# Where the tail of a rounded weight lies: two halves in PSUM, or one buffer in SBUF

## The chip, the core and the metric

The kernel runs on one core of a Trainium2 chip. The metric is the device time of one execution in microseconds (us): the lower the better. A core has TensorE (PE: matmuls and, beside them, PEld: the loads of their stationary operand), VectorE (DVE), ScalarE (ACT), GpSimd (POOL) and SyncE (SP), which here only issues DMAs. Each engine works through its own instructions in program order; semaphores hold an instruction until what it needs is done. SBUF is the working memory, PSUM the memory into which TensorE writes.

## What is computed

A linear attention with a decaying state (RWKV-6), for 4 batches, 8 heads, 768 tokens and a head size of 48, and then a two-layer network with SiLU on its output:

```python
for t in range(S):
    kt, vt, rt, wt = (k[:, :, t], v[:, :, t], r[:, :, t], w[:, :, t])
    cur = np.einsum('bhd,bhe->bhde', u[None] * kt, vt)
    y[:, :, t] = np.einsum('bhd,bhde->bhe', rt, state + cur)
    state = wt[:, :, :, None] * state + np.einsum('bhd,bhe->bhde', kt, vt)
x = y.transpose(0, 2, 1, 3).reshape(3072, 384)
h = x @ w_in                                   # 384 x 2048
g = h * (1.0 / (1.0 + np.exp(-h)))
out = g @ w_out                                # 2048 x 384
```

w_in and w_out come in as float64, everything else as float32. The kernel rounds the two weight matrices to float32 itself, from the two 32-bit words of each number. That rounding is what the change touches.

## The kernel before

The 768 tokens are cut into 6 blocks of 128; with 2 batches at a time this makes 12 **units**, `units[i]`. The attention of a unit (`mix(i)`) turns w, r and k so that channels lie on the partitions, and then goes through 7 **levels** (`level(i, l)`), in which the blocks of tokens that interact double in length. A level has 16 matmuls on TensorE (L377) that make scores; VectorE copies the masked scores out (L386, two of them), and multiplies r by the decay (L395, two inputs in SBUF); ScalarE copies half of the keys on (L365), and GpSimd multiplies the other half by the decay (L414, two of them). The next level's matmuls need L395, L365 and L414. In unit 1 GpSimd also has L333 and L334 (`bonus`), in unit 2 and later L322 (`products`).

The network of a unit has 8 steps `up(i, m)` (12 matmuls L549 each, SiLU on ScalarE at L552) and steps `down` (L559 for unit 0; for later units `quarter`, L604). `up(0, m)` is the first to use the m-th part of w_in, `down(0, ...)` the first to use w_out.

`merge` sets one program order for everything: each list of steps gets a stretch of a common time line, with unit i's attention at about i to i+1. The roundings of the 16 pieces of weight (0 to 7 of w_in, 8 to 15 of w_out) are put in at 0.6, from 1.0 to 1.83 and from 1.85 to 2.4, that is beside the levels of units 1 and 2; so are the steps `up(0, m)`, and `down(0, ...)` from 2.4 on.

One piece is 128 x 768 numbers of 64 bits. `round_weight(i)` issues, in this order: the add of any piece that is joined (`add_weight`), the join of piece i-1, the split of piece i, and the loads of later pieces into a place that is free by then.

- `split_weight(i)`: VectorE masks the high words into `head` (L169); ScalarE converts 16 bits of every number to `tail` (L173) and then works `head` over in place (L175). `head` lies in `temps[:, 0, i % 2]` in SBUF; `tail` in two PSUM tiles `p_o` of 384 columns, of which there are two in all.
- `join_weight(i)`: for each half, VectorE adds the low words to the tail in place (L189) and puts the sign bit on (L191), into `low`, `temps[:, 2, i % 2]` in SBUF.
- `add_weight()`: GpSimd adds `head` and `low`, both in SBUF, into the weight's place in `w_in_sb` or `w_out_sb` (L201). It is called ahead of each join and at the end of each level.

`temps` has room for three kinds of buffer, twice each; the kind with index 1 is not used by the rounding before. `p_o` is also the tile in which `down` and `quarter` gather their results, from `down(0, ...)` on. The later sums of Strassen's form (L578, L586) begin after the roundings.

Of the kernel before, what the change touches and what calls it, by code (L numbers as in the profile page):

```python
# [8 lines left out]
F32 = mybir.dt.float32  # L9
I8 = mybir.dt.int8  # L10
U16 = mybir.dt.uint16
U32 = mybir.dt.uint32
AF = mybir.ActivationFunctionType
ALU = mybir.AluOpType
# [19 lines left out]
def kernel(  # L34
# [11 lines left out]
    nc = tc.nc  # L46

    B, H, S, D = r.shape
    DM, DF = moe_w_in.shape
# [21 lines left out]
    ps = ctx.enter_context(tc.tile_pool(name="ps", bufs=1, space=bass.MemoryType.PSUM))  # L71
# [50 lines left out]
    PW = 2 * DM  # L122
# [17 lines left out]
    def staged(i):  # L140
        place = PLACES[i] - NOWN
        if place < 0:
            return own[:, PLACES[i]]
        return w_out_sb[:, 4 * place:4 * place + 4, :].rearrange("p a d -> p (a d)").bitcast(U32)
# [18 lines left out]
    half = {}  # L163
    temps = const.tile([128, 3, 2, PW], U32, name="temps")

    def split_weight(i):
        hi = staged(i)[:, 1::2]
        head = temps[:, 0, i % 2]
        nc.vector.tensor_scalar(out=head, in0=hi, scalar1=0x7FFF0000, scalar2=None, op0=ALU.bitwise_and)  # L169

        tails = [ps.tile([128, DM], F32, name="p_o", bufs=2) for x in range(PW // DM)]
        for x, tail in enumerate(tails):
            nc.scalar.activation(out=tail, in_=staged(i).bitcast(U16)[:, 2::4][:, x * DM:(x + 1) * DM],  # L173
                                 func=AF.Copy, scale=8.0)
        nc.scalar.activation(out=head, in_=head, func=AF.Relu, scale=8.0, bias=shift)  # L175
        half[i] = head, tails

    def join_weight(i):
        head, tails = half.pop(i)
        lo, hi = staged(i)[:, 0::2], staged(i)[:, 1::2]  # L180
        dst = w_ends[i][0].bitcast(U32)
        low = temps[:, 2, i % 2]

        def like(t):
            return t.rearrange("p (c f) -> p c f", c=dst.shape[1])

        for x, tail in enumerate(tails):
            part = slice(x * DM, (x + 1) * DM)
            nc.vector.scalar_tensor_tensor(out=tail.bitcast(U32), in0=lo[:, part], scalar=2.0 ** -29, in1=tail,  # L189
                                           op0=ALU.mult, op1=ALU.add)  # L190
            nc.vector.scalar_tensor_tensor(out=low[:, part], in0=hi[:, part], scalar=0x80000000, in1=tail.bitcast(U32),  # L191
                                           op0=ALU.bitwise_and, op1=ALU.bitwise_or)
        joined.append((dst, like(head), like(low)))

    joined = []
# [7 lines left out]
    def round_weight(i):  # L203

        add_weight()
        if rounded and 0 < i <= 2 * NW:
            join_weight(i - 1)
        if rounded and i < 2 * NW:
            split_weight(i)
        for j in due.get(i, ()):  # L210
            load_weight(j)
# [32 lines left out]
    for x, (c, p) in enumerate(parts):  # L244
        for e in range(2):
            first, rows = (2 * p + e) * D, slice(PD * e, PD * e + D)
            d0, d1 = max(0, c * 128 - first), min(D, (c + 1) * 128 - first)
            if d0 < d1:
                nc.scalar.copy(out=dense[rows, x, first + d0 - c * 128:first + d1 - c * 128],
                               in_=ident[rows, PD * e + d0:PD * e + d1])  # L250
# [4 lines left out]
    for l in range(NL):  # L255
# [3 lines left out]
        for b, sign in ((0, 1), (1, -1)):  # L259

            base, part = b * (L - 1), m[:, b]
# [428 lines left out]
```

## Time and profile before

| what | us |
|---|---|
| median of 3 runs (lowest, highest) | 744.31 (744.24, 745.98) |
| the profiled execution | 745.98 |
| its span, first to last instruction | 744.3 |
| TensorE busy in the span | 681.8 (92%) |
| VectorE, GpSimd, ScalarE busy | 441.1, 270.9, 174.7 |
| L189 and L191 (64 in all) | 35.4 |
| L173 (32 of them), L175 (16) | 16.3, 14.9 |
| L169 (16) | 13.1 |
| L201 (16) | 30.7 |

The rounding's instructions lie between 41 us (split of piece 0) and 151.6 us (add of piece 15). Lines of the profile name the line of the kernel, the engine, the operation and the operands as output<-inputs; a number after the last bar is the engine's idle time just ahead of such instructions, with what ended it. In a timeline each line starts with the start and the duration in us; `x2` means that two instructions were put together. In the chain of waits each line is a piece of the chain that ended last: start, length, engine and line.

### The profile page before, as it was taken

Reading aid. Unit: us, or ns where it says so; the run is one execution under the profiler, and the core shown is the slowest. Engines: PE = TensorE matmul, PEld = TensorE weight load, DVE = VectorE, ACT = ScalarE, POOL = GpSimd, SP = SyncE. Lnnn points to the kernel's source line nnn. Section 1 sums busy time; section 2 is a strip of 40 time slices with the busy share of each in tenths; the row PEclk is TensorE's granted clock in tenths of the full one; section 3 lists DMA queues with packets and bytes.
Section 4 is the critical chain, followed back from the end, with each engine's and each line's share of the span. In section 5 each row is a group of like instructions: output and inputs, shape, how many; then the busy total and the mean of one; then the engine's idle time right before and its main releaser. Section 6 shows DMA issues by size and latency. Waiting matters only on the chain.

```text
span 744.3 us, 12848 instructions
## 1 busy us (share of the span) xinstructions
PE 681.8 (92%) x4880; PEld 598.5 (80%) x4880; DVE 441.1 (59%) x783; ACT 174.7 (23%) x366; POOL 270.9 (36%) x376
## 2 busy tenths in 40 slices
PE   4584788399999999999999999999999999999998
PEld 3573666257988988988988988988988988988998
DVE  3746695977556656646646646756746747645122
ACT  4243444601202213112112113113112123022020
POOL 8725744570361351441442432431431441330000
PEclk9586789799999999999999999999999999999999
DMA  9904760554225234234144143143143020100000
GB/s 209 268 2 107 167 151 10 110 82 80 44 45 89 39 64 71 39 73 66 33 80 60 33 86 55 34 86 57 29 91 57 19 64 15 41 11 20 24 1 22
DMA packets 224239, 49.04 MB, mean 66 GB/s; under 512 B 212017, under 2 KB 219057, under 8 KB 224177
## 3 DMA queue, kind: packets, MB, share of 16 engines
q1 hardware_dynamic: 224032, 48.02, 33.5%
q8 instruction: 39, 0.64, 0.4%
q10 hardware_dynamic: 144, 0.20, 0.1%
q14 instruction: 24, 0.19, 0.1%
HBM read 39.52 MB, written 4.72 MB: 59 GB/s over the span
## 4 chain that ended last, share of the span: by engine, by line
PE 81%; DVE 9%; POOL 3%; ACT 2%; SPq 2%; issue 2%; DMA 1%; DVEq 0%; POOLq 0%
PE p_h L549 34%; PE p_o L604 24%; PE p_sc L377 11%; DVE score L386 4%; PE p_m L437 3%; PE p_m L445 3%; PE p_o L559 3%; DVE tr L395 2%; POOL tk L414 1%; DVE temps L191 1%; PE p_sc L459 1%; DVE p_o L189 1%; POOL w_in_sb L201 1%; ACT kq L424 1%; PE p_m L483 1%
## 5 line engine op out<-in xcount | busy, mean ns | idle before, releaser
L549 PE MATMUL p_h<-xt,w_in_sb 128*128 128x256 f32 x1152 | 276.7, 395 | 16.1 <-POOL w_in_sb L201 16.1
L549 PEld LDWEIGHTS p_h<-xt,w_in_sb 128*128 128x128 f32 x1152 | 220.8, 196 | 52.1 <-POOL w_in_sb L201 17.1
L386 DVE COPY_PREDICATED score<-mask,p_sc 128x512 f32<-128x512 int8 x162 | 133.4, 889 | 130.5 <-PE p_sc L377 130.5
L414 POOL TENSOR_TENSOR tk<-tk,tw 128x256 f32<-128x256 f32 x168 | 119.0, 730 | 213.1 <-PE p_sc L377 114.4
L552 ACT ACTIVATE gt<-p_h 128x512 f32<-128x512 f32 x96 | 57.1, 595 | 284.2 <-PE p_h L549 284.1
L377 PEld LDWEIGHTS p_sc<-tr,tk 48*128 48x128 f32 x1296 | 84.4, 197 | 48.3 <-issue 25.0
L377 PE MATMUL p_sc<-tr,tk 48*128 48x128 f32 x1296 | 100.2, 296 | 22.2 <-POOL tk L414 12.4
L604 PE MATMUL p_o<-w_out_sb,gt 128*128 128x192 f32 x528 | 90.3, 328 | 0.0
L604 PE MATMUL p_o<-own,temps 128*128 128x192 f32 x528 | 90.0, 328 | 0.0
L604 PEld LDWEIGHTS p_o<-w_out_sb,gt 128*128 128x128 f32 x528 | 86.2, 190 | 1.7
L604 PEld LDWEIGHTS p_o<-own,temps 128*128 128x128 f32 x528 | 85.9, 190 | 1.1
L395 DVE TENSOR_TENSOR tr<-tr,tw 128x512 f32<-128x512 f32 x82 | 65.7, 801 | 3.9 <-POOL ruk L333 2.2
L322 POOL TENSOR_TENSOR tw<-tw 128x512 f32<-128x512 f32 (+6 forms) x84 | 39.4, 468 | 75.3 <-DVE tw L298 66.8
L365 ACT COPY tk<-tk 128x256 f32<-128x256 f32 x72 | 32.7, 454 | 129.8 <-POOL tk L414 85.9
L464 POOL TENSOR_TENSOR state<-state,tw 128x512 f32<-128x512 f32 x16 | 16.3, 1041 | 87.8 <-PE p_m L437 87.8
L586 DVE TENSOR_TENSOR temps<-gt 128x256 f32<-128x256 f32 x88 | 36.9, 419 | 15.6 <-ACT gt L552 15.3
L613 DVE TENSOR_TENSOR ob<-p_o,partial 128x192 f32<-128x192 f32 x44 | 15.5, 352 | 39.5 <-PE p_o L604 39.4
L349 DVE COPY_PREDICATED score<-own_mask,diag 128x1024 f32<-128x1024 int8 x24 | 31.3, 1360 | 0.4
L604 PE MATMUL p_o<-w_out_sb,temps 128*128 128x192 f32 x176 | 31.3, 331 | 0.0
L604 PEld LDWEIGHTS p_o<-w_out_sb,temps 128*128 128x128 f32 x176 | 28.4, 190 | 1.1
L473 DVE TENSOR_TENSOR state<-p_sc,state 48x384 f32<-48x384 f32 x16 | 8.9, 555 | 32.9 <-PE p_sc L459 32.8
L334 POOL TENSOR_TENSOR ruk<-ruk,u_bc 128x384 f32<-128x384 f32 x24 | 26.0, 1081 | 1.9
(83 smaller groups left out, 563.5 us busy)
## 6 DMA issues: line engine op xcount, KB each, us to landing
out_dram<-ob SPq DMA_DIRECT2D x24, 192.0 KB, 1.9
w_out_sb<-in_moe_w_in_dram SPq DMA_DIRECT2D x5, 768.0 KB, 7.0
tokens_rk<-in_r_dram SPq DMA_DIRECT2D x10, 384.0 KB, 4.1
tokens_rk<-in_k_dram SPq DMA_DIRECT2D x10, 384.0 KB, 5.4
w_out_sb<-in_moe_w_out_dram SPq DMA_DIRECT2D x4, 768.0 KB, 4.9
own<-in_moe_w_out_dram SPq DMA_DIRECT2D x4, 768.0 KB, 5.2
xt<-yt SPq DMA_DIRECT2D x60, 48.0 KB, 2.0
raw<-in_w_dram SPq DMA_DIRECT2D x80, 32.0 KB, 2.2
```

The source lines that it names most:

```text
L322: nc.gpsimd.tensor_tensor(out=up, in0=t[:, :, 0::2], in1=t[:, :, 1::2], op=ALU.mult)
L334: nc.gpsimd.tensor_tensor(out=ruk[i, b], in0=ruk[i, b], in1=u_bc, op=ALU.mult)
L349: nc.vector.copy_predicated(out=score[:, i % NSC, e].rearrange("p (b q) t -> p b q t", b=NB), mask=own_mask[:, :, None, :].to_broadcast([1 ...
L365: nc.scalar.copy(out=keys(next_at * L + c, [4 * c, NP * ni // 2], [c, 2], [1, c]), in_=keys(c, [4 * c, NP * ni // 2], [NP * L + c, 2], [1, ...
L377: nc.tensor.matmul(bass.AP(tensor=s_p.tensor, offset=s_p.offset, ap=[s_p.ap[0], [apart * L // 2, 2], [1, L // 2]]), lhsT=tk[i][rows, x_at ...
L386: nc.vector.copy_predicated(out=dst, mask=masks[l][:, :, None].to_broadcast([128, NB, NP, ni, c]), data=sc[e].rearrange("p (b q) (i c) -> ...
L395: nc.vector.tensor_tensor(out=rb[:, :, :, 1, :], in0=rb[:, :, :, 1, :], in1=t[:, :, 0::2][:, :, :, None].to_broadcast([128, Q, ni, c]), op ...
L414: nc.gpsimd.tensor_tensor(out=out, in0=have, in1=odd, op=ALU.mult)
L549: nc.tensor.matmul(p_h[:, a, :], lhsT=w_in_sb[:, c, f * 128:(f + 1) * 128], rhs=xt[i][:, c, :], start=(c == 0), stop=(c == KC - 1))
L552: nc.scalar.activation(out=gt[i, m], in_=p_h, func=AF.Silu)
L586: nc.vector.tensor_tensor(out=out, in0=one, in1=two, op=op)
L604: nc.tensor.matmul(p, lhsT=left(f), rhs=right[:, f, :], start=(f == 0), stop=(f == FH - 1))
```

## The change

The tail of piece i moves from two PSUM tiles into `temps[:, 1, i % 2]`, in SBUF, as one buffer of 768 columns. So ScalarE writes it with one instruction instead of two, and the join has two VectorE instructions of 768 columns instead of four of 384. The first now writes `low` and reads the low words and the tail; the second puts the sign bit on `head`, in place, and not on the low part. GpSimd's add is as before, of `head` and `low`.

```diff
@@ def split_weight(i):
         nc.vector.tensor_scalar(out=head, in0=hi, scalar1=0x7FFF0000, scalar2=None, op0=ALU.bitwise_and)
-
-        tails = [ps.tile([128, DM], F32, name="p_o", bufs=2) for x in range(PW // DM)]
-        for x, tail in enumerate(tails):
-            nc.scalar.activation(out=tail, in_=staged(i).bitcast(U16)[:, 2::4][:, x * DM:(x + 1) * DM],
-                                 func=AF.Copy, scale=8.0)
+        tail = temps[:, 1, i % 2].bitcast(F32)
+        nc.scalar.activation(out=tail, in_=staged(i).bitcast(U16)[:, 2::4], func=AF.Copy, scale=8.0)
         nc.scalar.activation(out=head, in_=head, func=AF.Relu, scale=8.0, bias=shift)
-        half[i] = head, tails
+        half[i] = head, tail
@@ def join_weight(i):
-        head, tails = half.pop(i)
+        head, tail = half.pop(i)
         lo, hi = staged(i)[:, 0::2], staged(i)[:, 1::2]
...
-        for x, tail in enumerate(tails):
-            part = slice(x * DM, (x + 1) * DM)
-            nc.vector.scalar_tensor_tensor(out=tail.bitcast(U32), in0=lo[:, part], scalar=2.0 ** -29, in1=tail,
-                                           op0=ALU.mult, op1=ALU.add)
-            nc.vector.scalar_tensor_tensor(out=low[:, part], in0=hi[:, part], scalar=0x80000000, in1=tail.bitcast(U32),
-                                           op0=ALU.bitwise_and, op1=ALU.bitwise_or)
+        nc.vector.scalar_tensor_tensor(out=low, in0=lo, scalar=2.0 ** -29, in1=tail, op0=ALU.mult, op1=ALU.add)
+        nc.vector.scalar_tensor_tensor(out=head, in0=hi, scalar=0x80000000, in1=head,
+                                       op0=ALU.bitwise_and, op1=ALU.bitwise_or)
         joined.append((dst, like(head), like(low)))
```

## The prediction

> **What bounds the kernel now.** I read the slices of the page first, then the idle time of the costliest group, then the chain of waits and the timelines of VectorE (DVE) and GpSimd (POOL) over the first 160 us.
>
> ```profile
> PE   4584788399999999999999999999999999999998
> L549 PE MATMUL p_h<-xt,w_in_sb 128*128 128x256 f32 x1152 | 276.7, 395 | 16.1 <-POOL w_in_sb L201 16.1
> ```
>
> and of TensorE's timeline (start, duration, in brackets the idle time ahead):
>
> ```profile
> 142.27 3.82 PE L549 MATMUL p_h<-xt,w_in_sb 128*128 128x256 f32 x12
> 147.87 2.85 PE L559 MATMUL p_o<-w_out_sb,gt 128*128 128x384 f32 x8 [1.78 <-DVE temps L191]
> 152.30 1.16 PE L377 MATMUL p_sc<-tr,tk 48*128 48x128 f32 x16 [1.58 <-DVE tr L395]
> 153.39 5.43 PE L559 MATMUL p_o<-w_out_sb,gt 128*128 128x384 f32 x16
> ```
>
> From slice 9 on (about 150 us) TensorE is at 9 of 10: from 152.3 us to the end it hardly waits, so the end stands or falls with the moment at which the saturated part begins. Before that it waits for rounded weights (16.1 us for L201's adds into w_in_sb) and, last of all, 1.58 us for level 1's L395. A delay of that L395 is a delay of the end. What holds L395 back is the chain of waits:
>
> ```profile
> 140.20 1.79 POOL w_out_sb L201
> 141.99 0.02 issue
> 142.01 2.15 DVE temps L169
> ...
> 148.32 0.55 DVE temps L191
> 148.88 1.28 DVE score L386 x2
> ```
>
> The roundings run VectorE and GpSimd in alternation: between 120.9 and 152.2 us VectorE has only 1.1 us of idle, and GpSimd's add is what one of its instructions sits behind. How the two treat each other shows in their timelines (start, duration):
>
> ```profile
> 69.28 1.81 POOL L201 TENSOR_TENSOR w_in_sb<-temps 128x768 uint32<-128x768 uint32 x1
> 70.19 1.46 DVE L395 TENSOR_TENSOR tr<-tr,tw 128x512 f32<-128x512 f32 x1
> 71.04 1.47 POOL L333 TENSOR_TENSOR ruk<-raw 128x384 f32<-128x384 f32 x1
> ...
> 133.09 2.01 POOL L201 TENSOR_TENSOR w_out_sb<-temps 128x768 uint32<-128x768 uint32 x1 [2.68 <-DVE temps L191]
> 133.82 0.56 DVE L189 SCALAR_TENSOR_TENSOR p_o<-own,p_o 128x384 uint32<-128x384 uint32 x1
> 134.42 0.55 DVE L191 SCALAR_TENSOR_TENSOR temps<-own,p_o 128x384 uint32<-128x384 uint32 x1
> ```
>
> L395 has two SBUF inputs. It begins during an add, which ends at 71.09, and ends at 71.65, 0.55 us later; alone it takes about 0.69. GpSimd's next, L333, takes 1.47 where another of the same line takes 1.00 (at 80.39): it stood while L395 ran. So they take turns. L189 and L191 have one input in PSUM and keep their 0.55 in the midst of an add.
>
> **The skill.** "SBUF — State Buffer", section "Who interferes with whom": a DVE instruction with two SBUF inputs contends with a GpSimd instruction that reads SBUF; one with at most one SBUF input outside the two-port modes doesn't. Section "SBUF: two separate sides": the shared pair is an exclusive lock held for a whole instruction. The trace agrees in the lines above; L169 too, which has one source but passes 768 elements in 0.55 us and so is in a two-port mode, stands behind the add at 142.01 (2.15). "TensorE: Matmul & The Clock Gate", section "What's actually happening": after an idle window of about 3.4 us the clock is halved. Here: twelve L549 take 5.49 us at 80.48, after 3.75 us of idle, and 2.86 at 126.94.
>
> **The change part by part.** The diff holds one thing, whatever the title lists: the tail goes from two PSUM halves to one SBUF buffer.
>
> ScalarE: two L173 of 384 (0.52 each, 0.94 as a pair) become one of 768 into SBUF. Not in the trace: at best 0.80 (L313's 1.46 for 1536, less 768 elements at 0.86 ns, the step from L485's 384 in 479 ns to L424's 512 in 589), at worst 1.04, two apart; I take 0.9. L175 follows and waits for L169, so it is hidden either way. The 26.2 us that ScalarE waits for L191 to free PSUM between 50 and 200 us go; next is L175, which waits for L169 on VectorE, behind the same join. Nothing is gained but what the join gains.
>
> VectorE: four instructions of 384 become two of 768. 0.554 us for 384 is (384+148)/0.96 ns, so 768 take 0.95, and as they overlap by 0.08, a join of 1.74 replaces one of 2.12 (53.72 to 55.84): minus 0.38 where nothing contends. The second now reads head, so it waits for L175: that ran beside the first or long before.
>
> But each now reads two SBUF operands. Held by GpSimd, it ends 0.80 (768/0.96) after GpSimd's instruction, as L395's 512 did 0.55 after; held by it, an add (1.80 alone) ends some 1.74 after it. What is queued behind: on VectorE L169, then the level's L386 and L395, on which TensorE's next level waits; on GpSimd L201, on which L549 waits, and L414.
>
> The PSUM release: the 1.78 us of L559 go, but the next TensorE instruction, L377 at 152.30, waits for L395, so this is worth nothing. Weight loads on SP wait for the join that reads their place, and token loads queue behind: the last of these go out at 101.5 for transposes at 122, the last weight at 133.0 for use at 146.2. Some us of delay are covered.
>
> **Unit 1 (51 to 114 us), taking turns.** Join 0 runs alone: minus 0.38. Join 1 at 58.8 meets two L414 (0.67 each) and add 0: L414 to 59.5, first half 60.3, L414 60.97, second half 61.8, add 0 63.5 (before 62.15). L549 starts 1.36 late, and so does all behind it to level 2. Join 2 meets L333 and L334, and VectorE has 2.5 us of idle after it: covered. Add 2 still goes ahead of join 3, 81.8 against 80.42. Join 3 then takes turns with add 2, L333 and L334 (to 84.35, before 80.87), L169 follows at 85.7, add 3 at 87.45, join 4 with L414 to 89.65, add 4 at 92.45 (before 87.73). L549 had room there: its fifth group ends at 95.2, before 92.58. Join 5 ends at 95.8, add 5 at 98.0, add 6 at 103.55 (before 100.53), level 6's L386 starts at 111.3 (before 107.59), and the last L549 ends at 113.3, before 110.28. **Plus 3.0.**
>
> **Unit 2 (121 to 152 us), in the times of before.** Join 10 stands behind small L322 and makes them wait: ends as before, 127.8, but add 9 at 129.9 (before 128.64). L169 of weight 11 waits for it and for add 10: 132.1 (130.82). Join 11 alone: 133.8 (132.94). Join 12 stands behind add 11 (136.0): 137.7 (136.03); level 0 goes 1.65 late. Join 13 meets L414 and add 12: L414 to 141.85, half 142.65, add 144.4, half 145.2 (141.62). L169 then goes ahead of add 13, which saves its old stand of 1.6: 145.7 (144.16); add 13 to 147.4. Join 14: 148.2, 149.1 (146.28). Join 15 stands behind add 14 (151.3) and a L414: 153.6 (148.88). L386 follows, add 15 holds L395 to 156.6 (152.15). **Plus 4.45** where the saturated part begins.
>
> **Clock.** TensorE has done its L559 by 150.6 and stands about 6 us, against 1.58. A whole window of idle halves the clock for what comes next. Price: 5.49 less 2.86, **plus 2.6** for one such window. In unit 1 waits of such length are there already; I add nothing.
>
> Sum: 3.0 + 4.45 + 2.6 = 10.05. The profiled execution took 745.98 (span 744.3, so 1.7 around it): 756.0. The median of the three runs is 744.31, 1.67 below the profiled one, so 754.4; I say 754.
>
> Bounds: if VectorE keeps the port for both halves when GpSimd waits too, L395 in unit 2 ends at 154.4, but L414 of level 1 at 155, some 2.9 late in place of 4.45, and add 2 in unit 1 at 84.05, 3.6 late in place of 1.4: much the same. If no clock window is lost, 2.6 less. If waits in unit 1 open new ones (add 5 comes 1.7 us after its L549 could start), 2.6 to 5.2 more. So 749 to 759 for this case.
>
> **Rivals.** Mostly covered: the turns cost less than a whole instruction, and TensorE's waits in unit 1 take them up; only the +3 of unit 2 is left: 747.3. For it: 2.5 and 1.8 us of VectorE idle at levels 2 and 3. Against: none between 93.7 and 113.5 or after 121. Chance 0.12.
>
> Clock cascade: each late add costs a window more, +15 to +16: 760. For it: half the time between 55 and 144 us is at 0.5 already. Chance 0.08.
>
> Faster: the two-input form doesn't contend with the adds in unit 2, so that its joins keep 0.38 us less each. Six joins there (2.3), and joins 0, 1, 6 and 7 (some 1.1 in all): minus 3.4, 741. It decides if a join beside an add lasts under 2.12, the old length. For it: the trace shows the turns for L395 and L578 (2.57 beside an L333, 1.75 alone), never for this operation. Against: its inputs lie as theirs do. Chance 0.09. Gains and stands that cancel within 2 us: 0.03.
>
> **How the numbers follow.** Forecast 0.68, covered 0.12, cascade 0.08, faster 0.09, cancelled 0.03. A run tells 0.3% (2.2 us) from no change. Faster is the one case, 0.09; within 0.3% is the cancelled case and the edge of the covered one, 0.04; slower the rest, 0.87. The range of 747 to 759 leaves out the faster and the cancelled cases and most of the cascade, under 0.2.
>
> **What would show it.** Right: VectorE's joins at 0.95 alone and 1.5 to 2.7 beside an add; L201 with a mean over 2.0 (before 1.9); a longer TensorE wait for L395 near 157; a slice of half clock there; TensorE's busy part from there on as long as before. Wrong: joins of 0.95 in the midst of an add; or held joins with TensorE's saturated part beginning no later than 152.

## The result

| | median us (lowest to highest) | against before, 95% interval |
|---|---|---|
| before, 4 runs beside it | 744.59 (744.24 to 745.98) | |
| the change, 4 runs | 755.39 (754.19 to 756.71) | 1.0142 (1.0116 to 1.0167) |
| the change again, beside later experiments | 754.61 (754.12 to 756.69) | 1.0128 (1.0107 to 1.0150) |

The change makes the kernel 10.8 us slower (8.9 when measured again, against a before of 745.76): 755.39 us where 754 had been forecast. Beside the later runs with one half of the pieces, with four head buffers and with seven idle matmuls, 11 of the 42 executions of before took some 749 us and the others 745.3, so the ratios given for those four runs include both.

First the groups of the changed kernel's roundings (line, engine, operation, output<-inputs and shape, count; busy us, mean ns; idle ahead). L184 and L185 are the join's two instructions, L195 is GpSimd's add (L201 before):

```profile
L184 DVE SCALAR_TENSOR_TENSOR temps<-w_out_sb,temps 128x768 uint32<-128x768 uint32 x9 | 15.2, 1687 | 0.0
L184 DVE SCALAR_TENSOR_TENSOR temps<-own,temps 128x768 uint32<-128x768 uint32 x7 | 11.3, 1618 | 0.2 <-ACT temps L171 0.2
L185 DVE SCALAR_TENSOR_TENSOR temps<-w_out_sb,temps 128x768 uint32<-128x768 uint32 x9 | 11.3, 1255 | 0.0
L185 DVE SCALAR_TENSOR_TENSOR temps<-own,temps 128x768 uint32<-128x768 uint32 x7 | 10.1, 1444 | 0.1
L195 POOL TENSOR_TENSOR w_in_sb<-temps 128x768 uint32<-128x768 uint32 x8 | 17.0, 2126 | 2.7 <-DVE temps L185 2.7
L195 POOL TENSOR_TENSOR w_out_sb<-temps 128x768 uint32<-128x768 uint32 x8 | 16.2, 2024 | 10.5 <-DVE temps L185 10.5
```

Half the instructions take more time: 47.9 us in all where 64 took 35.4. 12 of the 32 last 0.92 to 0.96 us, as worked out for a join that isn't held; one takes 1.05; the other 19 take 1.37 to 2.57, all beside an instruction of GpSimd's. GpSimd's adds take 33.2 us in place of 30.7. Where the two engines meet shows in their timelines, VectorE's first (start, duration):

```profile
147.07 2.56 DVE L185 SCALAR_TENSOR_TENSOR temps<-own,temps 128x768 uint32<-128x768 uint32 x1
149.55 0.55 DVE L169 TENSOR_SCALAR temps<-w_out_sb 128x768 uint32<-128x768 uint32 x1
150.02 2.57 DVE L184 SCALAR_TENSOR_TENSOR temps<-w_out_sb,temps 128x768 uint32<-128x768 uint32 x1
152.51 0.95 DVE L185 SCALAR_TENSOR_TENSOR temps<-w_out_sb,temps 128x768 uint32<-128x768 uint32 x1
```

```profile
146.29 2.52 POOL L195 TENSOR_TENSOR w_out_sb<-temps 128x768 uint32<-128x768 uint32 x1
149.71 2.06 POOL L195 TENSOR_TENSOR w_out_sb<-temps 128x768 uint32<-128x768 uint32 x1 [0.90 <-DVE temps L185]
```

The add of 146.29 ends at 148.81, and the L185 that was issued at 147.07 ends 0.82 later. The add in turn takes 2.52 and not 1.80: it was issued while the join's first part was running (to 147.14). The same happens with L184 and the add of 149.71, which ends at 151.77; with nothing on GpSimd the next L185 takes 0.95. So here the two take turns by whole instructions.

The end of the chain of waits ahead of TensorE's saturated part (start, length, what) is the joins, one after another; what was L169 behind an add before is L184 and L185 behind instructions of GpSimd's now:

```profile
145.64 1.50 DVE temps L184
147.14 2.48 DVE temps L185
...
153.93 2.49 DVE temps L184
156.42 1.41 DVE temps L185
157.83 1.27 DVE score L380 x2
...
160.00 0.76 DVE tr L389
```

And TensorE's timeline at the same place:

```profile
152.71 2.74 PE L553 MATMUL p_o<-w_out_sb,gt 128*128 128x384 f32 x8
160.89 2.08 PE L371 MATMUL p_sc<-tr,tk 48*128 48x128 f32 x16 [5.44 <-DVE tr L389]
162.90 6.63 PE L553 MATMUL p_o<-w_out_sb,gt 128*128 128x384 f32 x16
169.46 1.16 PE L371 MATMUL p_sc<-tr,tk 48*128 48x128 f32 x16
```

The L553 no longer waits for PSUM, but level 2's L371 starts at 160.89 in place of 152.30, after 5.44 us of idle in place of 1.58, and it and the next 16 matmuls run slow (2.08 and 6.63 against 1.16 and 5.43); the profile's granted clock is 0.50 from 160.9 to 163.0, and 1.00 in before from 152.3 to 158.7. Then TensorE is saturated as before.

### The profile page after: what moved, and what is told of

Its sections match the earlier page's. It is cut to its first block, busy times and chain, and to the rows that moved or that the text cites. A ratio compares the mean times of both kernels' runs of the same rounds, so it can differ in the third digit from the quotient of the medians.

```text
span 755.0 us, 12803 instructions
## 1 busy us (share of the span) xinstructions
PE 684.3 (91%) x4880; PEld 600.2 (80%) x4880; DVE 450.8 (60%) x751; ACT 171.8 (23%) x350; POOL 282.3 (37%) x376
## 4 chain that ended last, share of the span: by engine, by line
PE 79%; DVE 9%; POOL 4%; ACT 3%; issue 2%; SPq 2%; DMA 1%; DVEq 0%; POOLq 0%; ACTq 0%
PE p_h L543 33%; PE p_o L598 24%; PE p_sc L371 11%; DVE score L380 4%; PE p_m L431 3%; PE p_m L439 3%; PE p_o L553 3%; DVE tr L389 2%; DVE temps L185 1%; POOL tk L408 1%; POOL w_in_sb L195 1%; DVE temps L184 1%; PE p_sc L453 1%; ACT gt L546 1%; ACT kq L418 1%
## 5 line engine op out<-in xcount | busy, mean ns | idle before, releaser
L543 PEld LDWEIGHTS p_h<-xt,w_in_sb 128*128 128x128 f32 x1152 | 221.1, 196 | 55.8 <-POOL w_in_sb L195 20.9
L408 POOL TENSOR_TENSOR tk<-tk,tw 128x256 f32<-128x256 f32 x168 | 124.9, 764 | 217.0 <-PE p_sc L371 117.6
L371 PEld LDWEIGHTS p_sc<-tr,tk 48*128 48x128 f32 x1296 | 84.9, 198 | 53.9 <-issue 24.9
L371 PE MATMUL p_sc<-tr,tk 48*128 48x128 f32 x1296 | 100.7, 297 | 27.8 <-POOL tk L408 12.6
L389 DVE TENSOR_TENSOR tr<-tr,tw 128x512 f32<-128x512 f32 x82 | 63.8, 778 | 3.9 <-POOL ruk L327 2.2
L580 DVE TENSOR_TENSOR temps<-gt 128x256 f32<-128x256 f32 x88 | 36.9, 419 | 15.6 <-ACT gt L546 15.3
L607 DVE TENSOR_TENSOR ob<-p_o,partial 128x192 f32<-128x192 f32 x44 | 15.5, 351 | 39.6 <-PE p_o L598 39.5
```

Source lines behind the costliest of these rows:

```text
L371: nc.tensor.matmul(bass.AP(tensor=s_p.tensor, offset=s_p.offset, ap=[s_p.ap[0], [apart * L // 2, 2], [1, L // 2]]), lhsT=tk[i][rows, x_at ...
L389: nc.vector.tensor_tensor(out=rb[:, :, :, 1, :], in0=rb[:, :, :, 1, :], in1=t[:, :, 0::2][:, :, :, None].to_broadcast([128, Q, ni, c]), op ...
L408: nc.gpsimd.tensor_tensor(out=out, in0=have, in1=odd, op=ALU.mult)
L543: nc.tensor.matmul(p_h[:, a, :], lhsT=w_in_sb[:, c, f * 128:(f + 1) * 128], rhs=xt[i][:, c, :], start=(c == 0), stop=(c == KC - 1))
L580: nc.vector.tensor_tensor(out=out, in0=one, in1=two, op=op)
```

## Experiments

To see which part of a run is longer, I cut each trace by TensorE's timeline at four points: the start of unit 1's level 0, the first matmul of unit 1's `y_state`, and the starts of levels 0 and 2 of unit 2.

| kernel | unit 1's levels | to unit 2's level 0 | level 0 to level 2 |
|---|---|---|---|
| before | 55.5 | 15.7 | 26.5 |
| the change | 58.3 | 16.7 | 30.8 |
| the change again | 56.1 | 16.7 | 30.8 |
| join in halves | 55.8 | 16.9 | 32.5 |
| sign on low | 56.6 | 16.9 | 31.0 |
| tail in PSUM, sign on head | 54.5 | 16.0 | 27.3 |
| pieces 0 to 7 alone | 57.3 | 17.2 | 26.5 |
| pieces 8 to 15 alone | 52.9 | 16.7 | 30.8 |
| four head buffers | 56.4 | 15.6 | 23.2 |
| before, adds on VectorE | 68.4 | 15.7 | 27.4 |
| the change, adds on VectorE | 66.2 | 15.5 | 25.1 |

**Is it the size of the instructions?**

```diff
-        nc.vector.scalar_tensor_tensor(out=low, in0=lo, scalar=2.0 ** -29, in1=tail, op0=ALU.mult, op1=ALU.add)
...
+        for x in range(2):
+            part = slice(x * DM, (x + 1) * DM)
+            nc.vector.scalar_tensor_tensor(out=low[:, part], in0=lo[:, part], scalar=2.0 ** -29, in1=tail[:, part],
+                                           op0=ALU.mult, op1=ALU.add)
...
```

> The changed kernel, but with the join in four VectorE instructions of 384 columns as before, still all in SBUF. Theory (turns: a join with two SBUF operands shares a port with GpSimd and each waits for whole instructions of the other): 9 to 14 us slower than before, since four held instructions a join offer more turns than two. Rival (size: it is the two long instructions that fit badly between the others): back to within 2 us of before.

755.93 us, 1.0139 (1.0113 to 1.0165) of before. Four instructions of 384 columns, as before the change, but in SBUF: the loss stays. So the size of the instructions isn't the cause. Level 0 to level 2 of unit 2 takes 32.5 us here, 1.7 more than in the change; that this comes from the greater number of turns is likely but not shown apart.

**Is it the new wait for ScalarE?**

```diff
-        nc.vector.scalar_tensor_tensor(out=head, in0=hi, scalar=0x80000000, in1=head,
+        nc.vector.scalar_tensor_tensor(out=low, in0=hi, scalar=0x80000000, in1=low,
```

> The changed kernel, but the sign bit goes onto the low part instead of head, so that the join doesn't read what ScalarE's second instruction (L175 of before) writes. Theory (turns): no more than 1.5 us off the changed kernel's 755.4. Rival (wait: the join's new wait for ScalarE is what costs): back to within 2 us of before's 744.6.

754.72 us, 1.0125 (1.0107 to 1.0144). Without that wait the loss is there as well.

**Half of the contending instructions.** Against the change; that the split writes its tail to two PSUM tiles, as before, is not printed here.

```diff
-        nc.vector.scalar_tensor_tensor(out=low, in0=lo, scalar=2.0 ** -29, in1=tail, op0=ALU.mult, op1=ALU.add)
+        for x, tail in enumerate(tails):
+            part = slice(x * DM, (x + 1) * DM)
+            nc.vector.scalar_tensor_tensor(out=low[:, part], in0=lo[:, part], scalar=2.0 ** -29, in1=tail,
+                                           op0=ALU.mult, op1=ALU.add)
         nc.vector.scalar_tensor_tensor(out=head, in0=hi, scalar=0x80000000, in1=head,
                                        op0=ALU.bitwise_and, op1=ALU.bitwise_or)
```

> The tail in two PSUM tiles as before, so that the join's first part has one SBUF operand, with the low part written to SBUF; the second part as in the change: one instruction of 768 on head, two SBUF operands, waiting for ScalarE. One contending instruction a join in place of two. Theory (turns): about half of the loss, 748 to 752. Rival (wait for ScalarE): the whole loss, 754 to 757. Rival (ScalarE's single tail instruction or its place costs): back to within 2 us of before.

748.89 us, 1.0045 (1.0028 to 1.0061): about a third of the loss, at the low end of what was expected of one contending instruction in two. In the same trace the instruction with its tail in PSUM isn't held, and the one with two SBUF operands is:

```profile
L191 DVE SCALAR_TENSOR_TENSOR temps<-own,temps 128x768 uint32<-128x768 uint32 x7 | 10.2, 1457 | 0.5 <-ACT temps L175 0.3
L189 DVE SCALAR_TENSOR_TENSOR temps<-own,p_o 128x384 uint32<-128x384 uint32 x14 | 7.0, 542 | 0.0
```

How much of the loss goes with half of the instructions this run tells only roughly. In its trace level 2 of unit 2 stands after a wait of 2.90 us, and it and the next 16 matmuls take 3.1 us more than the 1.16 and 5.43 of before, which is most of the 4.0 us between the two profiled executions:

```profile
153.18 2.08 PE L377 MATMUL p_sc<-tr,tk 48*128 48x128 f32 x16 [2.90 <-DVE tr L395]
155.19 7.57 PE L559 MATMUL p_o<-w_out_sb,gt 128*128 128x384 f32 x16
```

**Is GpSimd's add the partner?** Both kernels, with the adds on VectorE:

```diff
-            nc.gpsimd.tensor_tensor(out=dst, in0=head, in1=low, op=ALU.add)
+            nc.vector.tensor_tensor(out=dst, in0=head, in1=low, op=ALU.add)
```

> The kernel before with the 16 adds of head and low on VectorE in place of GpSimd, at the same points of the program[...]. It is there to be compared with the next run, the change with the same edit. VectorE has 16 instructions of some 0.95 us more: 3 to 12 us slower than before.

> The changed kernel with the same edit (adds on VectorE[...]). Theory (turns with GpSimd's add are most of the loss): with no add on GpSimd the change costs no more than 3 us against the run of the kernel before with the same edit, and may gain up to 3, as its joins are 0.38 us shorter where they meet nothing. Rival (the join's operands, sizes or waits cost by themselves): 8 us or more against that run, as without the edit.

With the edit the kernel before takes 759.08 us (1.0178, 1.0160 to 1.0196) and the changed one 758.49 (1.0169, 1.0153 to 1.0186). Both are slower, the first by 13.3 us where at most 12 had been expected, but the change now costs nothing: minus 0.6 us, where it costs 8.9 beside these runs (10.8 in the first measurement) with the adds on GpSimd. The joins of the changed kernel with this edit:

```profile
L184 DVE SCALAR_TENSOR_TENSOR temps<-w_out_sb,temps 128x768 uint32<-128x768 uint32 x9 | 9.4, 1047 | 0.0
L185 DVE SCALAR_TENSOR_TENSOR temps<-w_out_sb,temps 128x768 uint32<-128x768 uint32 x9 | 9.0, 1002 | 0.0
L185 DVE SCALAR_TENSOR_TENSOR temps<-own,temps 128x768 uint32<-128x768 uint32 x7 | 6.6, 948 | 0.0
L184 DVE SCALAR_TENSOR_TENSOR temps<-own,temps 128x768 uint32<-128x768 uint32 x7 | 6.6, 946 | 0.0
```

The same instructions on the same buffers: only 4 of the 32 are over 0.96 us, each of them beside another of GpSimd's instructions, and all take 31.7 us, less than the 35.4 of before. Nor does the extra time of the two kernels merely cover the loss: level 0 to level 2 of unit 2 is 25.1 us with the change and 27.4 without it, where with the adds on GpSimd it was 30.8 and 26.5. (After its wait of 3.2 us there TensorE runs slow again, which costs the change 2.9 us.) So it is the meeting with GpSimd's adds that makes the joins long and the change slow.

**Which pieces?** A condition chooses between the tail in SBUF and the two PSUM tiles, here for the first of two runs; in the second it is `i >= NW`:

```diff
+        if i < NW:
+            tail = temps[:, 1, i % 2].bitcast(F32)
...
```

> The change for pieces 0 to 7 (w_in, joined in unit 1) alone, pieces 8 to 15 with their tails in PSUM as before. Theory (turns; the sum's first term): plus 3 to 4 us over before, 747.6 to 748.6, with the last L549 of up(0) 2.8 to 3.3 us later than before. Rival (unit 1 has room that covers the turns, all of the loss arises in unit 2): within 1 us of before.

> The change for pieces 8 to 15 (w_out) alone, pieces 0 to 7 as before. Theory (turns; the sum's second term and the clock): plus 6 to 8 us over before, 750.6 to 752.6, and with the other half alone 10.7 in sum. Rival (the halves' losses aren't additive, since the second only begins where unit 1 is late): plus 3 us or less.

Pieces 0 to 7 alone: 748.34 us, 1.0032 (1.0019 to 1.0045). Pieces 8 to 15 alone: 751.27, 1.0066 (1.0037 to 1.0095). Each does cost: 2.9 and 5.8 us over the median of before beside them, 745.49. The first rival doesn't hold; the second is unlikely, as its 3 us lie at the low end of the interval (0.37%, or 2.8 us). Unit 2's stretch is 26.5 us in the first and 30.8 in the second, as in before and in the change, so its loss doesn't need a late unit 1. The sum of the two ratios, 1.0%, is under the whole's 1.3 to 1.4%. To see whether that means anything, the change once more:

> The changed kernel itself, beside the others of this call: 1.0 to 1.7% over before. If its two halves simply add up (0.3% and 0.7% measured), 1.0%; if the late start of unit 2 costs something of its own, 1.3% or more.

The ratio of 1.0128 (from 1.0107 on) lies nearer to the late start, but the ratios of the halves are held down by the executions of before near 749 us. By medians the halves cost 2.9 and 5.8 us, 8.6 together, and the change 8.9. So nothing here calls for a cost of the late start, though these runs can't exclude a small one.

**The clock.** Idle matmuls ahead of level 2 keep TensorE busy while it waits:

```diff
+        if (i, l) == (2, 2):
+            spare = ps.tile([128, DM], F32, name="p_m", bufs=2)
+            for x in range(12):
+                nc.tensor.matmul(spare, lhsT=ident, rhs=w_in_sb[:, 0, 0:DM], start=True, stop=True)
```

> The changed kernel with 12 idle matmuls of 384 columns (nothing reads what they write) ahead of unit 2's level 2, in TensorE's long wait for L395, so that the clock isn't halved there. Theory (of the loss, about 2 us are the half clock after that wait): L377 of that level takes 1.16 us again in place of 2.08, the next 16 matmuls of down 5.4 in place of 6.6, and the time is 753.3, 2 us under the changed kernel. Rival (the half clock only fills time that is lost anyway): no change within 0.7 us, or longer by up to 1 us.

754.87 us, 1.0131 (1.0108 to 1.0155): no gain, as the rival had it. TensorE's timeline says why:

```profile
155.26 7.90 PE L369 MATMUL p_m<-w_in_sb,ident 128*128 128x384 f32 x24
163.09 1.16 PE L376 MATMUL p_sc<-tr,tk 48*128 48x128 f32 x16
164.18 5.43 PE L558 MATMUL p_o<-w_out_sb,gt 128*128 128x384 f32 x16
```

The clock stayed up (1.16 and 5.43), but 12 matmuls are 24 passes of 0.33 us and kept level 2 back by 2.2 us, as much as they saved. With 7 of them:

> As the run with 12 idle matmuls, with 7: those 12 ran as 24 passes and 7.9 us and so ended 2.2 us after L395 was done, which ate what they saved. 7 of them take some 4.6 us and end before L395. Theory (2 us of the loss are half clock): 753.3, 2 us under the changed kernel. Rival (TensorE's clock is no part of it): within 0.7 us of the changed kernel.

```profile
152.91 4.68 PE L369 MATMUL p_m<-w_in_sb,ident 128*128 128x384 f32 x14
158.83 1.16 PE L376 MATMUL p_sc<-tr,tk 48*128 48x128 f32 x16 [1.25 <-DVE tr L394]
159.92 5.43 PE L558 MATMUL p_o<-w_out_sb,gt 128*128 128x384 f32 x16
```

752.3 us, 1.0082 (1.0057 to 1.0107). Against the change's 755.39 and 754.61 that is 2.3 to 3.1 us less; the interval of this ratio lies below that of the first and touches that of the second. In the trace the level and its 16 matmuls take 2.1 us less than in the first trace of the change and 1.8 less than in the second. So about a fifth of the loss is the slow clock after that wait.

**A use for the free buffer.** The kernel before has the same turns twice in unit 2, at 128.68 and 142.01 (2.15 us each): L169 waits for the add two pieces back, which frees its head buffer, and by then the next add is running. The buffer that the change takes for the tail can go to head:

```diff
-        head = temps[:, 0, i % 2]
+        head = temps[:, i // 2 % 2, i % 2]
```

> Not the change, but the kernel before with the buffer that the change takes (index 1 of temps) given to head instead: four head buffers, so that the split's L169 no longer waits for the add two pieces back, after which it stood behind the next add (2.15 us in place of 0.55, twice in unit 2). Theory (turns: a two-port L169 that starts earlier stands behind one add less): 1.5 to 3 us faster than before, 741.6 to 743.1. Rival (VectorE's next instructions only wait elsewhere): within 0.7 us of before.

742.45 us, 0.9947 (0.9933 to 0.9962): faster than both kernels, and 3.0 us under the median of before beside it. Level 0 to level 2 of unit 2 takes 23.2 us in place of 26.5. The L169 that took 2.15 us at 142.01, after a wait of 0.39, is now

```profile
140.87 0.79 DVE L169 TENSOR_SCALAR temps<-w_out_sb 128x768 uint32<-128x768 uint32 x1
```

since it waits for no add, begins near the end of one (139.42 to 141.24) and runs ahead of the next. The one at 128.7 takes 1.15.

## Why the prediction was right

The two profiled executions differ by 10.74 us in span (755.00 and 744.26), the sum had 10.05. Term by term:

- **A join of two SBUF operands takes turns with GpSimd.** Right, and shown: by the durations, and by the adds on VectorE (minus 0.6 us in place of 8.9); the smaller loss with half of the contending instructions agrees. The price of a turn was right too: 0.95 alone, and 0.80 to 0.83 after the end of the add. The 1/0.96 = 1.04 ns a column on which it rests comes out of the lines of before: L613 takes 352 ns for 192 columns and L191 554 for 384, which is 1.05 ns a column.
- **Unit 2, plus 4.45.** Measured 4.33 (26.47 to 30.80), and the same again in two other runs. The working holds step by step. Level 0 starts 4.26 us later than in before (130.09 and 125.83); set that much later, join 13 should end at 149.5, join 15 at 157.9 and L395 at 160.9, and they end at 149.6, 157.8 and 160.8.
- **Unit 1, plus 3.0.** Measured 2.8 in this pair of traces; but the second trace of the same changed kernel gives 0.65, and the run with pieces 8 to 15 alone, whose pieces 0 to 7 are those of before, is 2.6 us quicker in unit 1 than before. What differs is where TensorE runs slow. What the groups of 12 L549 take above 2.86 us and those of 16 L377 above 1.16 adds up to 9.4 us of this stretch in before and 7.0 with pieces 8 to 15 alone, and to 8.7 and 5.7 in the two traces of the change. Without it the stretch is 46.1 and 45.9, and 49.6 and 50.4. So, as an estimate, the turns cost 3.5 to 4.5 us in unit 1, more than the 3.0, and the slow clock costs 0.7 to 3.7 us less than in before, where the prediction added nothing and so kept every slow L549. One of those is gone in both traces of the change, with a shorter wait ahead of it (before, then the change):

```profile
100.59 5.49 PE L549 MATMUL p_h<-xt,w_in_sb 128*128 128x256 f32 x12 [2.73 <-POOL w_in_sb L201]
105.40 2.86 PE L543 MATMUL p_h<-xt,w_in_sb 128*128 128x256 f32 x12 [1.44 <-POOL w_in_sb L195]
```

That the two errors nearly cancel in this pair is luck, and so the sum was luckier than its parts.
- **Clock, plus 2.6.** Measured 2.1: L371 0.92 and 16 L553 1.20 us longer; 1.8 in the second trace. The price had been taken from twelve L549; the mechanism was right.
- **Left out, plus 1.0.** Between unit 1's `y_state` and unit 2's level 0 the change is 1.0 us longer. The prediction costed ScalarE's L175 at nothing. It is L172 now, waits for L169 behind the joins, and the copies of y to SBUF stand in its queue:

```profile
116.42 0.94 ACT L172 ACTIVATE temps<-temps,shift 128x768 uint32<-128x768 uint32 x1 [5.22 <-DVE temps L169]
117.26 0.58 ACT L546 ACTIVATE gt<-p_h 128x512 f32<-128x512 f32 x1
117.73 1.06 ACT L443 COPY yt<-p_m 128x512 f32<-128x512 f32 x2
```

for which TensorE's L477 waits 1.16 us. The prediction saw that ScalarE's wait would move to L169, but not what was queued behind it at that place. That this move is the cause isn't shown: with pieces 0 to 7 alone, where ScalarE writes the tails of pieces 8 and 9 to PSUM as before, the same wait is 1.55 us. What both have in common, and the run with pieces 8 to 15 alone (1.16) too, is that join 8 starts 0.7 us after unit 1's `y_state`, where in before it starts 1.3 us ahead of it.
- The remaining 0.5 us are there before the first join: level 0 of unit 1 starts at 55.09, not 54.63. The other traces have it between 53.5 and 55.4, so this is most likely spread; but the first split stands ahead of it (in before from 27 us on, not from 41 as is said above), so a part of the change in it isn't excluded.
- **The PSUM release is worth nothing.** Right: the 1.78 us went, and L371's wait for L395 (L389 now) grew from 1.58 to 5.44.
- **Rivals.** The faster case would have needed joins of 0.95 in the midst of an add; there are none in the trace. The covered case fails by unit 2, which passes its 4.3 us on in full.

## What to carry to other kernels

Before an operand is moved from PSUM to SBUF, count the SBUF operands of the VectorE instruction that reads it and look at what GpSimd does at that time: with two, each of the engines may stand for a whole instruction of the other, and here fewer instructions, 1.74 us a join in place of 2.12 where nothing is met, didn't make up for that. The trace of the kernel as it is shows the price, if any other instruction with two SBUF operands overlaps GpSimd. Here the spare buffer was better spent on the instruction that came late for its turn (L169, 3.0 us).

## What the runs showed of the hardware that was not expected

Executions of one and the same kernel differ in where TensorE's clock is halved: the levels of unit 1 took 58.3 us in one trace of the changed kernel and 56.1 in another, with each join the same to within 0.02 us. The times of the change lie in two groups to match, five of eight at 754.1 to 755.0 us and three at 756.4 to 756.7. So of a stretch like this one, with waits of 3 to 5 us on TensorE, one trace tells the time to no better than some 2 us, unless the slow matmuls are counted apart. The slow clock also followed waits shorter than the window of 3.4 us that the prediction goes by: 2.73 us ahead of the L549 at 100.59 in before, and 2.90 with the tail in PSUM and the sign on head. And a 128x384 float32 matmul stands in the trace as two passes of 0.33 us each (24 for 12), which has to be counted when idle matmuls are to fill a gap.
